# Cached attention, one core: the output projection cut at 24 rows instead of 28, with two transposed tail blocks

## The chip, the cores and the metric

The kernel runs on one core of a Trainium2 chip. The metric is device time in microseconds (us), lower is better: the median of several executions. A profile is one execution recorded instruction by instruction. Engines are named as the profile names them: PE (TensorE, matrix products), PEld (its loads of the stationary operand), DVE (VectorE), ACT (ScalarE), POOL (GpSimd), SP (SyncE, which here issues nearly all DMA transfers). All inputs and the output are bf16; sums are kept in fp32.

## The reference

One new token for each of 32 sequences attends over the last 512 positions of a cache of 2048. There are 32 query heads and 8 key/value heads, so four query heads share one key head.

```python
B, Sq, D = x.shape                 # 32, 1, 512
Hq, Dh = 32, 128
W = min(4096, max(256, Sk // 4))   # 512
q = (x @ wq).reshape(B, Sq, Hq, Dh).transpose(0, 2, 1, 3)
k = jnp.repeat(k_cache[:, :, Sk - W:, :], rep, axis=1)
v = jnp.repeat(v_cache[:, :, Sk - W:, :], rep, axis=1)
p = softmax(einsum("bhqd,bhkd->bhqk", q, k) * Dh ** -0.5)
o = einsum("bhqk,bhkd->bhqd", p, v)
return o.transpose(0, 2, 1, 3).reshape(B, Sq, Hq * Dh) @ wo     # [32, 4096] @ [4096, 512]
```

The last line is the output projection, the part that the change cuts differently. Its contraction is over 4096 = 32 heads of 128, so each row of the output sums 32 products.

## The kernel before, in words

**Data.** One batch's window of keys is 8 heads x 512 positions x 128 numbers, 1 MB; so is its window of values. With 32 batches and two weights of 4 MB the core reads 75.5 MB. SP issues the loads in one written-out order: `k(b)` and `v(b-3)` in turn up to b = 28, with `wo` after b = 10, then `k` of 29 to 31, then `v` of 26 to 31. A key load waits until PE has transposed the keys four batches earlier (four buffers); a value load waits until PE has used the values ten batches earlier (ten buffers). The two output transfers stand behind all of these on SP.

**One batch on PE.** `transposes(b)` turns a batch's keys in 32 products of 128x128 (line 218) into four PSUM banks of `kT_ps`; DVE copies three of the four banks to SBUF and ACT the fourth (lines 416 and 353). `scores(b)` is 8 products of 128x512 (line 234).

**One block is four batches.** The scores of four batches (4 x 32 rows) accumulate in one half of `sc_ps`, the halves taken in turn: even blocks use columns 0 to 511, odd blocks 512 to 1023. When block `kb` is complete, DVE takes its row maximum (`max_block`, lines 438 and 440), ACT the exponential with the row sum (`exp_block`, 365), DVE the reciprocal and the scaling (`norm_block`, 445 and 449), PE transposes the probabilities (`ptrans`, 248), ACT copies them (`pt_evac`, 379), PE multiplies by the values (`pv`, 32 narrow products of 128x4 for each batch, line 263), and DVE copies the block's result to `oT_sb` (`ot_evac`, 456). `oT_sb` holds the attention output transposed: a head's 128 numbers on the partitions, a column for each batch and head.

**The output projection.** Two forms are used. In `oproj_main` (line 279) the attention output is the stationary operand and a head's 128x512 slice of `wo` streams past: 32 products give the first 28 rows of the output directly, in `sc_ps[0:28, 0:512]`. In `oproj_last` (line 292) a 128x128 piece of `wo` is stationary and the last block's 4 columns stream past: 4 x 32 = 128 narrow products give the last 4 rows transposed, in 16 columns of `m_ps`; DVE copies them (466), PE turns them in 4 transposes (302), DVE copies them again (468), and SP writes them out (166).

**Order.** Every engine has its own program, written out by hand; semaphores join them, and an engine stands at a wait until it is met. In PE's loop, step s does `transposes(s+2)`, `scores(s)`, and, where a block is due, `ptrans` and `pv`. The loop runs to s = 27, and the end before the change is lines 317 to 332. Written with T for transposes and S for scores: T30, S28, ptrans(6), S29, pv(6) of batches 0 and 1, T31, S30, pv(6) of batches 2 and 3, S31, `oproj_main`, ptrans(7), pv(7), `oproj_last`. `oproj_main` waits for `ot_evac(6)`, which DVE's program puts behind `max_block(7)` (lines 497 and 498).

Of the kernel before, what the change touches and what calls it, by code (L numbers as in the profile page):

```python
# [5 lines left out]
B = 32  # L6
D = 512
H = 32
G = 8
REP = H // G  # L10
DH = 128
SK = 2048
W = 512
# [9 lines left out]
WO_AFTER = 10  # L23
LAG1 = 1
LAG2 = 2

BF16 = mybir.dt.bfloat16
FP32 = mybir.dt.float32
# [5 lines left out]
def bass_standalone__sliding_block_cached__sampling_kernel(  # L34
# [5 lines left out]
    wo: bass.AP,  # L40
    out: bass.AP,
):
    scale = float(DH) ** -0.5
    with ExitStack() as ctx:
        sb = lambda name, shape, dt: ctx.enter_context(nc.sbuf_tensor(name, shape, dt))
# [14 lines left out]
        oT_sb = sb("oT_sb", [128, B * H], BF16)  # L60
        out_sb = sb("out_sb", [128, D], BF16)
        out_sb2 = sb("out_sb2", [128, D], BF16)
        oT2_sb = sb("oT2_sb", [128, 16], BF16)
        mx = [sb(f"mx{i}", [128, 8], FP32) for i in range(2)]
        nmx = [sb(f"nmx{i}", [128, 8], FP32) for i in range(2)]
        ssum = [sb(f"ssum{i}", [128, 8], FP32) for i in range(2)]
# [44 lines left out]
        @block.sync  # L111
        def _(sp):
            def load_k(b):
                slot = b % NK
                if b >= NK:
                    sp.wait_ge(sem_pe_kT, 4 * (b - NK) + 4)
                src = k_cache[b, :, SK - W:, :].rearrange("g (p r) d -> p g (r d)", p=128)
                dst = kbuf[slot][:, :].rearrange("p (g x) -> p g x", g=G)
                sp.dma_start(dst, src).then_inc(sem_k[slot], 16)  # L119

            def load_v(b):
                slot = b % NV
                if b >= NV:
                    sp.wait_ge(sem_pe_pv, b - NV + 1)
                src = v_cache[b, :, SK - W:, :].rearrange("g (p r) d -> p g (r d)", p=128)
                dst = vbuf[slot][:, :].rearrange("p (g x) -> p g x", g=G)
                sp.dma_start(dst, src).then_inc(sem_v[slot], 16)

            def load_wo():
                sp.wait_ge(sem_pe_misc, 2)  # L130
                sp.wait_ge(sem_act_misc, 2)
                sp.dma_start(
                    wbuf[:, :].rearrange("p (h n) -> p h n", h=H),
                    wo.rearrange("(h p) n -> p h n", p=128),
                ).then_inc(sem_wo, 16)

            NB_LAST = B - 4
            load_k(0)
            sp.dma_start(  # L139
                wbuf[:, :].rearrange("p (t n) -> p t n", t=DT),  # L140
                wq.rearrange("(t p) n -> p t n", p=128),
            ).then_inc(sem_wq, 16)
            order = []
            for b in range(1, NB_LAST + 1):
                order.append(("k", b))
                if b >= VLAG:
                    order.append(("v", b - VLAG))
                if b == WO_AFTER:
                    order.append(("wo", 0))
            for b in range(NB_LAST + 1, B):  # L150
                order.append(("k", b))
            for b in range(NB_LAST + 1 - VLAG, B):
                order.append(("v", b))
            assert len(order) == len(set(order)) == 2 * B
            for kind, b in order:
                if kind == "k":
                    load_k(b)
                elif kind == "v":
                    load_v(b)
                else:  # L160
                    load_wo()
            outv = out.rearrange("b o d -> (b o) d")
            sp.wait_ge(sem_dve_out, 1)
            sp.dma_start(outv[0:NB_LAST, :], out_sb[0:NB_LAST, :]).then_inc(sem_out, 16)
            sp.wait_ge(sem_dve_out, 3)
            sp.dma_start(outv[NB_LAST:B, :], out_sb2[0:B - NB_LAST, :]).then_inc(sem_out, 16)
            sp.wait_ge(sem_out, 32)

        @block.gpsimd
# [12 lines left out]
        def _(pe):  # L182
# [38 lines left out]
            def scores(b):  # L221
                blk, bl = divmod(b, 4)
                half = blk % 2
                if bl == 0:
                    pe.wait_ge(sem_dve_L, blk + 1)
                    if blk == 0:
                        pe.wait_ge(sem_act_misc, 2)
                    if blk >= 2:
                        pe.wait_ge(sem_act_exp, blk - 1)
                for g in range(G):  # L230
                    n = 4 * b + g // 2
                    if g % 2 == 0:
# [36 lines left out]
                            )  # L269
                    ins.then_inc(sem_pe_pv, 1)  # L270

            NB_LAST = B - 4

            def oproj_main():
                pe.wait_ge(sem_dve_oT, NBLK - 1)
                pe.wait_ge(sem_wo, 16)
                pe.wait_ge(sem_act_exp, NBLK - 1)
                for h in range(H):
                    ins = pe.matmul(  # L279
                        sc_ps[0:NB_LAST, 0:512],  # L280
                        bass.AP(oT_sb, h, [[B * H, 128], [H, NB_LAST]]),
                        wbuf[:, h * D:(h + 1) * D],
                        start=(h == 0),
                        stop=(h == H - 1),
                    )
                ins.then_inc(sem_pe_misc, 1)

            def oproj_last():
                pe.wait_ge(sem_dve_oT, NBLK)
                for c in range(4):  # L290
                    for h in range(H):
                        ins = pe.matmul(  # L292
                            m_ps[:, c * 4:(c + 1) * 4],
                            wbuf[:, h * D + c * 128: h * D + (c + 1) * 128],
                            bass.AP(oT_sb, NB_LAST * H + h, [[B * H, 128], [H, B - NB_LAST]]),
                            start=(h == 0),
                            stop=(h == H - 1),
                        )
                ins.then_inc(sem_pe_misc, 1)
                pe.wait_ge(sem_dve_out, 2)  # L300
                for c in range(4):
                    ins = pe.transpose(pT_ps[0:B - NB_LAST, c * 128:(c + 1) * 128], oT2_sb[:, c * 4:(c + 1) * 4], ident[:, :])  # L302
                ins.then_inc(sem_pe_misc, 1)

            xT()
            transposes(0)
            transposes(1)
            qproj()
            for s in range(0, NB_LAST):
                transposes(s + 2)  # L310
                scores(s)
                for kb in range(NBLK - 2):
                    if s == 4 * kb + 3 + LAG1:
                        ptrans(kb)
                    if s == 4 * kb + 3 + LAG2:
                        pv(kb)
            transposes(NB_LAST + 2)
            scores(NB_LAST)
            ptrans(NBLK - 2)
            scores(NB_LAST + 1)  # L320
            pv(NBLK - 2, (0, 1))
            transposes(NB_LAST + 3)
            scores(NB_LAST + 2)
            pv(NBLK - 2, (2, 3))
            scores(NB_LAST + 3)
            oproj_main()
            ptrans(NBLK - 1)
            pv(NBLK - 1, (0,))
            pv(NBLK - 1, (1,))
            pv(NBLK - 1, (2,))  # L330
            pv(NBLK - 1, (3,))
            oproj_last()

        @block.scalar
        def _(act):
# [42 lines left out]
                    act.wait_ge(sem_act_pT, kb - 1)  # L378
                act.activation(pT_sb[kb % 2][:, :], pT_ps[:, 0:W], ACTF.Copy).then_inc(sem_act_pT, 1)  # L379

            def block_tasks_pre(b):
                pass

            def block_tasks_post(b):
                for kb in range(NBLK):
                    if b == 4 * kb + 5:
                        exp_block(kb)
                    if b == 4 * kb + 5 + LAG1:
                        pt_evac(kb)

            xt_evac()
            evac(0, 3)
            evac(1, 3)
            qt_evac()
            for b in range(2, B):
                block_tasks_pre(b)
                evac(b, 3)
                block_tasks_post(b)
            for b in range(B, B + 12):
                block_tasks_pre(b)  # L400
                block_tasks_post(b)

        @block.vector
        def _(dve):
# [50 lines left out]
                reg = kb % 4  # L455
                dve.tensor_copy(oT_sb[:, kb * 128:(kb + 1) * 128], m_ps[:, reg * 128:(reg + 1) * 128]).then_inc(sem_dve_oT, 1)  # L456

            NB_LAST = B - 4

            def out_evac():  # L460
                dve.wait_ge(sem_pe_misc, 3)
                dve.tensor_copy(out_sb[0:NB_LAST, :], sc_ps[0:NB_LAST, 0:512]).then_inc(sem_dve_out, 1)

            def out_last():
                dve.wait_ge(sem_pe_misc, 4)
                dve.tensor_copy(oT2_sb[:, :], m_ps[:, 0:16]).then_inc(sem_dve_out, 1)
                dve.wait_ge(sem_pe_misc, 5)
                dve.tensor_copy(out_sb2[0:B - NB_LAST, :], pT_ps[0:B - NB_LAST, 0:512]).then_inc(sem_dve_out, 1)

            def E(b):  # L470
                for c in range(3):
                    evac(b, c)

            def block_tasks_pre(b):
                for kb in range(NBLK):
                    if b == 4 * kb + 6 and kb <= NBLK - 2:
                        norm_block(kb)
                    if b == 4 * kb + 5 + LAG2 + 1 and kb <= NBLK - 3:
                        ot_evac(kb)

            def block_tasks_post(b):
                for kb in range(NBLK - 1):
                    if b == 4 * kb + 5:
                        max_block(kb)
                for blk in range(1, NBLK):
                    if b == max(2, 4 * blk - 2):
                        lcopy(blk)

            E(0)
            E(1)  # L490
            lcopy(0)
            for b in range(2, B):
                block_tasks_pre(b)
                E(b)
                block_tasks_post(b)
            kb6, kb7 = NBLK - 2, NBLK - 1
            max_block(kb7)
            ot_evac(kb6)
            norm_block(kb7)
            out_evac()  # L500
            ot_evac(kb7)
            out_last()


# [26 lines left out]
```

## Time and profile before

| | |
|---|---|
| median of 6 runs | 235.33 us (234.91 to 237.51) |
| the profiled execution's own time | 236.34 us |
| its span, first to last instruction | 234.2 us |
| mean granted PE clock | 0.85 |
| busy: PE / PEld / DVE / ACT | 176.4 / 137.8 / 78.9 / 46.3 us |
| read from HBM | 75.53 MB, 323 GB/s over the span |
| `oproj_main`: 32 products, start to start of the next work | 215.67 to 222.78 us |
| `oproj_last`: 128 narrow products | 227.65 to 231.24 us |

How to read it: times inside the trace are us from the first instruction. A busy share is an average over the span; the end of this kernel has a limit of its own, so a stage is read by itself. The chain of work that ended last is followed back from the last instruction, at each step to whatever released it. The start and end of PE's instructions overlap, since products are pipelined; the pace of a group is the distance between starts. The granted clock is the share of full speed that PE was given.

### The profile page before, as it was taken

What the parts mean: (1) busy time and instruction counts of PE and PEld (TensorE: products, weight loads), DVE (VectorE), ACT (ScalarE), POOL (GpSimd) and SP (SyncE); (2) the same over time, 40 slices, a digit from 0 to 9 for tenths busy, and PEclk for the clock granted to TensorE, in tenths of its full rate; (3) what the DMA queues carried; (4) which work ended last, traced back from release to release, by engine and by line L of the source; (5) the groups of instructions that cost most, each with busy time, mean ns of one, the idle gap of its engine ahead of it and who ended that gap; (6) DMA issues with size and microseconds to landing.
All of it is one profiled execution on the core that took longest, in us unless ns stands there. A gap on an engine that the chain in (4) does not pass through costs nothing.

```text
span 234.2 us, 5764 instructions
## 1 busy us (share of the span) xinstructions
PE 176.4 (75%) x2609; PEld 137.8 (59%) x2632; DVE 78.9 (34%) x147; ACT 46.3 (20%) x59; POOL 8.2 (4%) x9
## 2 busy tenths in 40 slices
PE   0606799699863029996968679977998699997985
PEld 0506767468641026964846459745875588675575
DVE  0303335442361003444333531553165306632011
ACT  2100232221132001034111410332023101511010
POOL 7600000000000000000000000000000000000000
PEclk9965999899799556799997977997799778999975
DMA  6999999999999999999999999999999999999200
GB/s 230 413 391 348 350 349 349 350 348 350 348 351 348 348 348 350 348 350 348 349 350 348 349 348 349 348 349 348 350 348 348 348 348 347 350 335 345 82 8 4
DMA packets 71306, 75.94 MB, mean 324 GB/s; under 512 B 1090, under 2 KB 70754, under 8 KB 70770
## 3 DMA queue, kind: packets, MB, share of 16 engines
q1 hardware_dynamic: 71250, 75.53, 100.0%
q8 instruction: 21, 0.34, 0.6%
q0 software_dynamic: 32, 0.03, 0.0%
q14 instruction: 3, 0.02, 0.0%
HBM read 75.53 MB, written 0.03 MB: 323 GB/s over the span
## 4 chain that ended last, share of the span: by engine, by line
DMA 51%; PE 42%; issue 3%; DVE 1%; SPq 0%; ACT 0%; DVEq 0%
DMA kbuf<-in_k_cache_dram 51%; PE kT_ps L218 16%; PE sc_ps L234 12%; PE m_ps L263 9%; PE sc_ps L279 3%; PE m_ps L292 2%; PE sc_ps L195 1%; DVE kT L416 1%; DVE mx L438 0%; ACT pT L379 0%; DVE oT_sb L456 0%; PE pT_ps L302 0%; PE pT_ps L248 0%; SPq L139 0%; SPq L119 0%
## 5 line engine op out<-in xcount | busy, mean ns | idle before, releaser
L218 PE MATMUL kT_ps<-ident,kbuf 128*128 128x128 bf16 x1024 | 79.1, 249 | 43.8 <-DMA kbuf<-in_k_cache_dram 42.0
L218 PEld LDWEIGHTS kT_ps<-ident,kbuf 128*128 128x128 bf16 x1024 | 74.0, 114 | 50.5 <-DMA kbuf<-in_k_cache_dram 46.6
L416 DVE COPY kT<-kT_ps 128x1024 bf16<-128x1024 bf16 x96 | 62.4, 686 | 83.0 <-issue 40.2
L234 PE MATMUL sc_ps<-kT,L 128*128 128x512 bf16 x233 | 60.2, 398 | 2.0 <-issue 0.9
L353 ACT ACTIVATE kT<-kT_ps 128x1024 bf16<-128x1024 bf16 x32 | 32.7, 1023 | 140.0 <-PE kT_ps L218 129.1
L234 PEld LDWEIGHTS sc_ps<-kT,L 128*128 128x128 bf16 x256 | 24.9, 103 | 26.2 <-issue 5.5
L263 PEld LDWEIGHTS m_ps<-pT,vbuf 128*128 128x128 bf16 x1024 | 27.2, 97 | 2.7 <-ACT pT L379 0.9
L263 PE MATMUL m_ps<-pT,vbuf 128*128 128x4 bf16 x1024 | 27.2, 165 | 0.7 <-ACT pT L379 0.7
L456 DVE CAST oT_sb<-m_ps 128x128 bf16<-128x128 f32 x8 | 2.3, 292 | 36.1 <-PE m_ps L263 36.1
L438 DVE TENSOR_REDUCE mx<-sc_ps 128x1 f32<-128x512 f32 x8 | 5.5, 692 | 12.8 <-PE sc_ps L234 12.8
L365 ACT ACTIVATE E_sb<-sc_ps,nmx 128x512 f32<-128x512 f32 x8 | 5.5, 687 | 15.9 <-DVE nmx L440 15.9
L279 PE MATMUL sc_ps<-wbuf,oT_sb 128*28 128x512 bf16 x32 | 7.1, 380 | 1.2 <-DVE oT_sb L456 1.2
L379 ACT ACTIVATE pT<-pT_ps 128x512 bf16<-128x512 bf16 x8 | 4.8, 597 | 13.1 <-PE pT_ps L248 13.1
L279 PEld LDWEIGHTS sc_ps<-wbuf,oT_sb 128*28 128x28 bf16 x32 | 3.9, 126 | 4.4 <-DVE oT_sb L456 1.7
L187 PE MATMUL pT_ps<-ident,x_sb 32*128 32x32 bf16 x4 | 0.3, 183 | 7.2 <-DMA x_sb<-in_x_dram 7.2
L187 PEld LDWEIGHTS pT_ps<-ident,x_sb 32*128 32x128 bf16 x4 | 0.2, 101 | 7.2 <-issue 7.2
L449 DVE TENSOR_SCALAR P<-E_sb,rs 128x512 bf16<-128x512 f32 x8 | 3.9, 487 | 0.3
L292 PE MATMUL m_ps<-oT_sb,wbuf 128*128 128x4 bf16 x128 | 3.6, 168 | 0.4 <-DVE oT_sb L456 0.4
L292 PEld LDWEIGHTS m_ps<-oT_sb,wbuf 128*128 128x128 bf16 x128 | 3.5, 103 | 0.5 <-DVE oT_sb L456 0.5
L430 DVE COPY L<-qT_sb 128x128 bf16<-128x128 bf16 x8 | 2.1, 259 | 4.5 <-ACT qT_sb L342 4.5
L248 PEld LDWEIGHTS pT_ps<-ident,P 128*128 128x128 bf16 x32 | 2.4, 98 | 2.1 <-issue 0.4
L445 DVE RECIPROCAL rs<-ssum 128x1 f32<-128x1 f32 x8 | 1.3, 164 | 6.5 <-ACT E_sb L365 6.5
(22 smaller groups left out, 26.1 us busy)
## 6 DMA issues: line engine op xcount, KB each, us to landing
kbuf<-in_k_cache_dram SPq DMA_DIRECT2D x32, 1024.0 KB, 12.0
vbuf<-in_v_cache_dram SPq DMA_DIRECT2D x32, 1024.0 KB, 12.1
wbuf<-in_wq_dram SPq DMA_DIRECT2D x1, 4096.0 KB, 15.2
wbuf<-in_wo_dram SPq DMA_DIRECT2D x1, 4096.0 KB, 20.8
x_sb<-in_x_dram POOLq DMA_DIRECT2D x1, 32.0 KB, 5.9
out_dram<-out_sb SPq DMA_DIRECT2D x1, 28.0 KB
out_dram<-out_sb SPq DMA_DIRECT2D x1, 4.0 KB
```

Of the source, the lines that this page charges most:

```text
L218: ins = pe.transpose(dst, src, ident[:, :])
L234: ins = pe.matmul(sc_ps[:, half * 512:(half + 1) * 512], L[blk % 2][:, (bl * 8 + g) * 128:(bl * 8 + g + 1) * 128], kT_sb[b % NKT][:, g * W ...
L248: ins = pe.transpose(pT_ps[:, j * 128:(j + 1) * 128], P_sb[kb % 2][:, j * 128:(j + 1) * 128], ident[:, :])
L263: ins = pe.matmul(m_ps[:, reg * 128 + bl * 32 + 4 * g: reg * 128 + bl * 32 + 4 * g + 4], vbuf[vslot][:, g * W + j * 128: g * W + (j + 1) * ...
L279: ins = pe.matmul(sc_ps[0:NB_LAST, 0:512], bass.AP(oT_sb, h, [[B * H, 128], [H, NB_LAST]]), wbuf[:, h * D:(h + 1) * D], start=(h == 0), st ...
L292: ins = pe.matmul(m_ps[:, c * 4:(c + 1) * 4], wbuf[:, h * D + c * 128: h * D + (c + 1) * 128], bass.AP(oT_sb, NB_LAST * H + h, [[B * H, 12 ...
L353: act.activation(kT_sb[b % NKT][:, c * 1024:(c + 1) * 1024], kT_ps[:, bank * 1024:(bank + 1) * 1024], ACTF.Copy,).then_inc(sem_act_kT, 1)
L365: act.activation(E_sb[:, :], sc_ps[:, half * 512:(half + 1) * 512], ACTF.Exp, bias=nmx[kb % 2][:, 0:1], scale=1.0, accum_out=ssum[kb % 2][ ...
L379: act.activation(pT_sb[kb % 2][:, :], pT_ps[:, 0:W], ACTF.Copy).then_inc(sem_act_pT, 1)
L416: dve.tensor_copy(kT_sb[b % NKT][:, c * 1024:(c + 1) * 1024], kT_ps[:, bank * 1024:(bank + 1) * 1024],).then_inc(sem_dve_kT, 1)
L438: dve.tensor_reduce(mx[kb % 2][:, 0:1], sc_ps[:, half * 512:(half + 1) * 512], AXX, ALU.max).then_inc(sem_dve_loc, 1)
L449: dve.tensor_scalar(P_sb[kb % 2][:, :], E_sb[:, :], rs[kb % 2][:, 0:1], None, ALU.mult).then_inc(sem_dve_P, 1)
```

## The change

The direct form now makes 24 rows (blocks 0 to 5) and is called `oproj_A`; it writes the other half of `sc_ps` (columns 512 to 1023) and stands on PE right after S27. Blocks 6 and 7 each get the transposed form, `oprojT(6)` and `oprojT(7)`, 128 narrow products each, into 32 columns of `m_ps`; one `out_transposes` turns both together, and the second output transfer carries 8 rows. PE's end becomes T28, S26, S27, `oproj_A`, ptrans(6), pv(6) of batches 0 and 1, T29, S28, T30, T31, S29, S30, S31, pv(6) of batches 2 and 3, `oprojT(6)`, ptrans(7), pv(7), `oprojT(7)`, `out_transposes`. S28 gets one more wait, for DVE's copy of `oproj_A`'s result, since block 7 uses that half of `sc_ps`. On DVE the end is written out: E28 (three bank copies), max and norm of block 6, the copy of `oproj_A`'s result, E29 to E31, `ot_evac(6)`, max and norm of block 7, `ot_evac(7)`. ACT keeps the same operations: E28, exp and probabilities of block 6, E29 to E31, the same for block 7. The order of the loads on SP is the same list as before.

```diff
-        oT2_sb = sb("oT2_sb", [128, 16], BF16)
+        oT2_sb = sb("oT2_sb", [128, 32], BF16)
...
-            sp.dma_start(outv[0:NB_LAST, :], out_sb[0:NB_LAST, :]).then_inc(sem_out, 16)
+            sp.dma_start(outv[0:NB_A, :], out_sb[0:NB_A, :]).then_inc(sem_out, 16)
             sp.wait_ge(sem_dve_out, 3)
-            sp.dma_start(outv[NB_LAST:B, :], out_sb2[0:B - NB_LAST, :]).then_inc(sem_out, 16)
+            sp.dma_start(outv[NB_A:B, :], out_sb2[0:B - NB_A, :]).then_inc(sem_out, 16)
...
+                    if b == NB_A + 4:
+                        pe.wait_ge(sem_dve_out, 1)
...
+            def oproj_A():
+                pe.wait_ge(sem_dve_oT, NB_A // 4)
                 pe.wait_ge(sem_wo, 16)
+                pe.wait_ge(sem_act_exp, NB_A // 4)
                 for h in range(H):
                     ins = pe.matmul(
+                        sc_ps[0:NB_A, 512:1024],
+                        bass.AP(oT_sb, h, [[B * H, 128], [H, NB_A]]),
                         wbuf[:, h * D:(h + 1) * D],
...
+            def oprojT(kb):
+                pe.wait_ge(sem_dve_oT, kb + 1)
+                q = kb - (NBLK - 2)
                 for c in range(4):
                     for h in range(H):
                         ins = pe.matmul(
+                            m_ps[:, c * 8 + 4 * q: c * 8 + 4 * q + 4],
                             wbuf[:, h * D + c * 128: h * D + (c + 1) * 128],
+                            bass.AP(oT_sb, 4 * kb * H + h, [[B * H, 128], [H, 4]]),
...
+            transposes(28)
+            scores(26)
+            scores(27)
+            oproj_A()
+            ptrans(6)
+            pv(6, (0, 1))
+            transposes(29)
+            scores(28)
+            transposes(30)
+            transposes(31)
+            scores(29)
+            scores(30)
+            scores(31)
+            pv(6, (2, 3))
+            oprojT(6)
+            ptrans(7)
+            pv(7, (0,))
...
+            oprojT(7)
+            out_transposes()
...
+            ot_evac(5)
+            E(28)
+            max_block(6)
+            norm_block(6)
+            out_evac_A()
+            E(29)
+            E(30)
+            E(31)
+            ot_evac(6)
+            max_block(7)
+            norm_block(7)
+            ot_evac(7)
             out_last()
```

## The prediction

> **What bounds the kernel now.** I read the page's 40 slices first, because a busy share over the whole span cannot say what bounds the end.
>
> ```profile
> PE   0606799699863029996968679977998699997985
> ...
> PEclk9965999899799556799997977997799778999975
> DMA  6999999999999999999999999999999999999200
> ```
>
> One slice is 5.9 us. The transfers are saturated from slice 1 to slice 36, that is to about 217 us, and PE has holes among them. In slices 32 to 39, about 188 us on, PE shows no low digit. So there may be a handover: transfers set the pace for most of the span, and PE sets it before the transfers have ended. The chain of work that ended last says where. Its last piece of transfer is the key load that releases T27 at 183.76 us; from there to the end every piece is compute (columns: start us, length us, what).
>
> ```profile
> 195.38 1.67 PE sc_ps L234 x7
> 197.06 1.79 PE kT_ps L218 x32
> 198.84 1.73 PE sc_ps L234 x8
> ...
> 214.52 0.70 DVE mx L438
> ...
> 215.67 7.11 PE sc_ps L279 x32
> ...
> 223.80 3.48 PE m_ps L263 x128
> 227.30 0.30 DVE oT_sb L456
> ...
> 227.65 3.59 PE m_ps L292 x128
> ```
>
> The reader is to see that S26, T29 and S27 follow each other without a hole, and that nothing between 195 and 214 us waits for a load: PE is full there, at granted clock 1.00. Idle time of PE begins only after S31, and it is small: 214.49 to 215.67 (DVE's maximum, its negation and ot_evac(6)), then 223.12 to 223.80 (ACT's copy of the probabilities), then 227.28 to 227.65 (ot_evac(7)). The chain also has a piece of 2.13 us called "issue" at 206.05, which would be a hole if it were empty. The timeline (start, length, engine, line, operation) shows PE at work in it:
>
> ```profile
> 205.87 1.75 PE L263 MATMUL m_ps<-pT,vbuf 128*128 128x4 bf16 x64
> ```
>
> and the 32 products of T31 start at 207.48. It is not idle time.
>
> **The move of the large block.** oproj_main costs 7.11 us for 32 products of 512 columns, 222 ns each. oproj_A has the same 32 products with 24 instead of 28 stationary columns. Their loads take 125 ns (line 279's weight loads, median) and lie under the 222 ns, so I give the smaller block no gain: 7.11 us leaves the tail and 7.11 us enters between S27 and ptrans(6). Its waits are met there: block 5's exp and ot_evac (192.38 to 192.67 us) are long done at 198.8 us. PE has no hole to put it in, so all that follows, T29 to S31 and pv(6), starts 7.11 us later than its own work would allow. **Cost 0.** The cover that could make it a gain would be PE waiting for keys 29 to 31 in that stretch; no such wait is recorded before T29, T30 or T31.
>
> **The second tail block.** oprojT(6) is new work on PE: 128 products like line 292's, while row count in the direct form fell without making it shorter. Line 292 took 3.59 us for 128, at clock 0.50. The same shape in pv(6) at clock 1.00 took 1.58 us for 64, that is 3.16 us for 128. Ends 3.16 and 3.59; it starts around 223 us, and in the run of before the clock fell at 225.4, so I take **+3.5**.
>
> **The wait after ptrans(6).** Before, ACT's copy of block 6's probabilities lay beside S29 (1.74 us) and PE did not stand. Now pv(6) follows ptrans(6) at once. The row for it is the same step of block 7: 223.12 to 223.80, 0.02 + 0.60 + 0.05. Queued behind pv(6) on PE are T29 and everything to the end. **+0.67.** With something put between, it would be 0.
>
> **The wait before oprojT(6).** It needs ot_evac(6), which needs the end of pv(6). The row is ot_evac(7), 227.28 to 227.65: **+0.39** (its idle time on PE in the timeline; 0.37 by the chain).
>
> **The wait that goes.** After S31 PE stood 214.49 to 215.67, **-1.18**. Late next is block 7's softmax, which DVE now starts only after ot_evac(6). From the start of the maximum (214.52) to the end of the scaling (216.44 + 0.49 = 216.93) it takes 2.41 us. Counted from the end of pv(6): 0.35 + 2.41 = 2.8 us, against 0.39 + 3.5 = 3.9 us until oprojT(6) ends. So it is hidden by oprojT(6) with 1.1 us to spare; without that cover ptrans(7) would stand for up to 2.8 us.
>
> **DVE and ACT around the moved block.** DVE's copy of oproj_A's result (0.68 us, line 462's row) now stands ahead of E29 to E31, and DVE waits at it for oproj_A. Behind it wait T30 and S29 at most; it ends about 206.6 us by my schedule, and T29's first bank is complete only after 208.9. S28's new wait is for the same copy and is met 3 us earlier. T30 and T31 now come back to back: six DVE copies of 0.63 us (1.89 for three), 3.8 us, against 3.6 to 3.9 us of transposes, with S29 needing E29 only. **0**, between 0 and 0.4. The first output transfer moves to about 207 us, but on SP it still stands behind the last value load; 24 KB at the 349 GB/s of those slices is 0.07 us, and pv(7) starts some 6 us after the transfers have faded (slices of 0.5 us: 0.22 at 218.5, then almost nothing). **0**; if a load had to wait for it, 0.07.
>
> **The end.** oT2 is 32 columns instead of 16: line 456 takes 292 ns for 128 columns and line 466 about 177 for 16, a slope of 1 ns, so +0.02. The 4 KB transfer becomes 8 KB; the tail from its issue to the end is 234.2 - 232.56 = 1.6 us for 4 KB and I give the other 4 KB nothing (a gain is excluded, the amount is twice; a loss is at most 0.02 at 349 GB/s). ptrans(7) follows some 6 us of narrow products instead of the wide oproj_main, so it may find the clock at 0.50, as the last four transposes did (0.60 us against 0.35): **+0.2**, with pv(7)'s first half, between 0 and 0.4.
>
> **Code.** PE gets 256 more instructions. The trace has one stall inside a group of transposes without a releaser, 1.82 us at 27.74 us, right after the 128 products of the query projection. The nearest rows, pv(7) and oproj_last with 128 products each, have none. I take 0, between 0 and 1.82.
>
> **Sum:** 3.5 + 0.67 + 0.39 - 1.18 + 0.02 + 0.2 = **+3.6 us**. On the profiled execution's own time, 236.34, this gives 239.9; that execution stands 1.0 above the median of the runs, so on 235.33 it gives **238.9**.
>
> **The clock.** The granted clock moves in steps of 3.41 us. The rows are windows cut on those steps (PE busy, PEld, DVE, ACT, POOL, then granted clock, DMA share, GB/s):
>
> ```profile
> 112.80:116.21 3.41, 3.36 (x97) 2.76 (x96) 0.22 (x1) 0.69 (x1) 0.00 (x0) 1.00 1.09 349
> 116.21:119.62 3.41, 3.36 (x79) 3.06 (x77) 2.06 (x4) 0.44 (x1) 0.00 (x0) 1.00 1.12 353
> ...
> 187.89:191.30 3.41, 3.36 (x100) 2.82 (x100) 0.00 (x0) 0.00 (x0) 0.00 (x0) 1.00 1.10 348
> 191.30:194.72 3.42, 3.42 (x65) 3.42 (x62) 1.60 (x3) 0.00 (x0) 0.00 (x0) 0.50 1.10 348
> ...
> 222.02:225.43 3.41, 2.72 (x73) 2.06 (x72) 0.68 (x1) 0.60 (x1) 0.00 (x0) 1.00 0.03 8
> 225.43:228.85 3.42, 3.03 (x114) 2.95 (x112) 0.29 (x1) 0.00 (x0) 0.00 (x0) 0.50 0.02 5
> ```
>
> Narrow products and idle time together fill 2.27 us of the window at 112.80 (pv starts at 113.94) and the clock stays. They fill 2.36 us at 187.89 (pv from 188.94) and 2.3 us at 222.02 (0.68 idle, pv from 223.80), and it falls to 0.50 for the next step. In the new order ptrans(6)'s wait and pv(6) of two batches make 0.67 + 1.6 to 1.75, about 2.3 to 2.4 us, between oproj_A and T29. That is at the boundary, and only if one window holds all of it. By the phase of this run a step would end at 208.37 and hold about 2.1 of it. If the clock falls, T29 and S28 run at half speed for one step, at most 3.41 / 2 = 1.7 us. I take 0, with 1.7 as the far end.
>
> [...]
>
> **The rivals.** (a) As summed, 238.9 us: chance 0.66. (b) The clock falls after pv(6), 238.9 + 1.5 = 240.4 us (T29 at up to 3.60 us, as the transposes at 86.48 in the chain, instead of 1.79; the cap of 1.7 for one step, less a little for a step that ends or begins in other work): for it the 2.3 against 2.27 us; against it that the phase must fit, (3.41 - 2.35) / 3.41 = 0.3. Chance 0.22. (c) Part of the chain's "issue" piece is real idle time that the new order fills: 238.9 - 2.1 = 236.8 us; against it the 64 products recorded there. Chance 0.05. (d) Faster, by one mechanism: in 195 to 214 us PE in truth stands for keys 29 to 31, and oproj_A lies beside that wait. If all 7.11 us are hidden, 238.9 - 7.1 = 231.8 us; it decides the sign as soon as 3.6 us are hidden. For it: transfers run at 348 GB/s to 216 us. Against it: clock 1.00 with PE busy 4.95 of 5 us at 195 to 200 and 200 to 205. Chance 0.04. (e) The change does nothing that can be measured, its added work eaten by the 1.18 us and a shorter oproj_A: it would need 24 stationary columns to cost 3.6 us less than 28. Chance 0.03.
>
> **How the numbers follow.** About 0.5% (1.2 us) is what a measurement of this kernel can tell from no change. Slower: (a) + (b) + (c) = 0.93 ((c) lies 0.6% above). Faster: (d) 0.04. Same: (e) 0.03. The low end of (a) has oprojT(6) at 3.16 and the clock effect of the end at 0: 3.16 + 0.67 + 0.39 - 1.18 = 3.0, and from it the spread of the runs below their median (0.42) is taken: 237.9. The high end takes in (b) with its far end 1.7: 235.33 + 5.3 = 240.6, and 0.1 for the stalls bounded above. The range 237.9 to 240.7 leaves out (c), (d) and (e), 0.12.
>
> **What the next profile would show.** Right: in the chain, line of oproj_A directly after S27 at about 199 us with no hole before it; PE idle about 0.67 us before pv(6) and 0.4 before oprojT(6); oprojT twice, 256 products; S31 ending about 6.2 us later than 214.49 (7.11 + 0.67, less the 1.6 of pv(6) that now follows it); the last DVE copy about 3.6 us later. Wrong: holes of PE before T29 to T31 that end on a load (then (d)); T29 at 3 us or more (then (b)); ptrans(7) waiting for DVE's scaling (then the cover of block 7's softmax is gone, up to 2.8 us more).

## The result and the profile after

The changed kernel is slower: 240.65 us median (239.55 to 242.17) against 235.36 us, a ratio of 1.022 (95% interval 1.018 to 1.026). A second comparison gave 239.96 against 235.45 us, 1.0186 (1.0136 to 1.0236). So the change costs 4.5 to 5.3 us. The forecast was 238.9 us with a range of 237.9 to 240.7.

The profiled execution took 240.36 us, with a span of 237.3 us. Its slices (5.9 us each) that answer to those shown of before:

```profile
PE   0606699669952049966976699669886999899985
...
PEclk9999999997999558998899997999599999979855
DMA  7999999999999999999999999999999999998000
```

The transfers end in the same place, at about 218 us. In the stretch where PE is full, from about 190 us on, one slice of the clock stands out: a 7 in slice 35 (207.7 to 213.6 us), which the windows below resolve. (The 5 in slice 28, from 166 us, lies ahead of T27.) The chain of waits of the changed kernel from the large block on (start us, length us, what):

```profile
196.33 7.04 PE sc_ps L280 x32
203.36 0.34 PE pT_ps L251 x4
203.71 0.02 issue
203.73 0.61 ACT pT L390
204.34 0.05 issue
204.38 1.76 PE m_ps L266 x64
206.14 2.55 PE kT_ps L219 x32
208.68 0.22 issue
208.91 2.42 PE sc_ps L237 x7
...
220.08 1.60 PE m_ps L266 x64
221.68 0.02 issue
221.70 0.30 DVE oT_sb L464
222.01 0.05 issue
222.05 3.55 PE m_ps L294 x128
```

The reader is to see five things. The large block now stands at 196 us and is as long as before (7.04 against 7.11 us). After ptrans(6) PE waits 0.67 us for ACT's copy. Before the new 128 products it waits 0.37 us for DVE's copy. The new products take 3.55 us. And T29 and S28 take 2.55 and 2.42 us, where the kernel before had 1.79 and 1.68 us for the same work. The windows of the changed kernel, cut at the steps of the clock (PE busy, PEld, DVE, ACT, POOL, granted clock, DMA share, GB/s), show why:

```profile
203.59:207.00 3.41, 2.72 (x84) 2.62 (x83) 0.79 (x2) 0.60 (x1) 0.00 (x0) 1.00 1.09 348
207.00:210.42 3.42, 3.20 (x21) 2.22 (x20) 1.58 (x3) 1.02 (x1) 0.00 (x0) 0.50 1.06 344
210.42:213.83 3.41, 3.41 (x52) 2.95 (x51) 1.96 (x4) 0.62 (x1) 0.00 (x0) 1.00 1.05 344
```

The first window holds the 0.69 us of idle time and the narrow products of pv(6) whole, and the clock is 0.50 for the step that follows.

### The profile page after: what moved, and what is told of

The parts are those of the page before. It is cut to its first block, busy times and chain, and to the rows that moved or that the text cites. A ratio compares the mean times of both kernels' runs of the same rounds, so it can differ in the third digit from the quotient of the medians.

```text
span 237.3 us, 6022 instructions
## 1 busy us (share of the span) xinstructions
PE 174.2 (73%) x2738; PEld 135.1 (57%) x2760; DVE 78.4 (33%) x147; ACT 46.4 (20%) x59; POOL 8.2 (3%) x9
## 4 chain that ended last, share of the span: by engine, by line
DMA 56%; PE 37%; issue 3%; DVE 2%; ACT 1%; SPq 0%; DVEq 0%
DMA kbuf<-in_k_cache_dram 56%; PE kT_ps L219 11%; PE sc_ps L237 11%; PE m_ps L266 8%; PE m_ps L294 3%; PE sc_ps L280 3%; PE sc_ps L196 1%; DVE kT L424 1%; ACT pT L390 1%; PE pT_ps L251 0%; DVE oT_sb L464 0%; PE pT_ps L306 0%; SPq L140 0%; SPq L121 0%; DVE out_sb L474 0%
## 5 line engine op out<-in xcount | busy, mean ns | idle before, releaser
L219 PE MATMUL kT_ps<-ident,kbuf 128*128 128x128 bf16 x1024 | 73.6, 239 | 49.2 <-DMA kbuf<-in_k_cache_dram 46.7
L219 PEld LDWEIGHTS kT_ps<-ident,kbuf 128*128 128x128 bf16 x1024 | 68.2, 108 | 56.6 <-DMA kbuf<-in_k_cache_dram 52.4
L424 DVE COPY kT<-kT_ps 128x1024 bf16<-128x1024 bf16 x96 | 61.6, 686 | 86.5 <-issue 38.1
L237 PE MATMUL sc_ps<-kT,L 128*128 128x512 bf16 x234 | 58.6, 391 | 1.9 <-issue 0.4
L294 PE MATMUL m_ps<-oT_sb,wbuf 128*128 128x4 bf16 x256 | 7.1, 168 | 0.8 <-DVE oT_sb L464 0.8
L294 PEld LDWEIGHTS m_ps<-oT_sb,wbuf 128*128 128x128 bf16 x256 | 7.0, 101 | 0.9 <-DVE oT_sb L464 0.9
L280 PE MATMUL sc_ps<-wbuf,oT_sb 128*24 128x512 bf16 x32 | 7.1, 380 | 0.0
L280 PEld LDWEIGHTS sc_ps<-wbuf,oT_sb 128*24 128x24 bf16 x32 | 3.7, 119 | 3.3 <-issue 0.4
L179 POOL MEMSET L<- 128x4096 bf16 x1 | 3.5, 3507 | 0.0
L180 POOL MEMSET L<- 128x4096 bf16 x1 | 3.5, 3507 | 0.0
```

What stands on the lines that cost most here:

```text
L179: pool.memset(L[0][:, :], 0.0).then_inc(sem_pool, 1)
L219: ins = pe.transpose(dst, src, ident[:, :])
L237: ins = pe.matmul(sc_ps[:, half * 512:(half + 1) * 512], L[blk % 2][:, (bl * 8 + g) * 128:(bl * 8 + g + 1) * 128], kT_sb[b % NKT][:, g * W ...
L280: ins = pe.matmul(sc_ps[0:NB_A, 512:1024], bass.AP(oT_sb, h, [[B * H, 128], [H, NB_A]]), wbuf[:, h * D:(h + 1) * D], start=(h == 0), stop= ...
L294: ins = pe.matmul(m_ps[:, c * 8 + 4 * q: c * 8 + 4 * q + 4], wbuf[:, h * D + c * 128: h * D + (c + 1) * 128], bass.AP(oT_sb, 4 * kb * H + ...
L424: dve.tensor_copy(kT_sb[b % NKT][:, c * 1024:(c + 1) * 1024], kT_ps[:, bank * 1024:(bank + 1) * 1024],).then_inc(sem_dve_kT, 1)
```

## The experiments

All times below are medians, with the ratio to the kernel before, measured beside it, and its 95% interval.

| kernel | us | ratio | interval |
|---|---|---|---|
| changed, again | 239.96 | 1.0186 | 1.0136 to 1.0236 |
| wait after ptrans(6) filled | 238.97 | 1.0131 | 1.0077 to 1.0186 |
| T29 into that wait | 238.37 | 1.0098 | 1.0063 to 1.0133 |
| T29 into that wait, and pv(5) cut in two | 238.23 | 1.0088 | 1.0053 to 1.0123 |
| T29 ahead of S27, T30 into that wait | 239.24 | 1.0159 | 1.0138 to 1.0181 |
| one tail block | 240.51 | 1.0173 | 1.0115 to 1.0230 |
| one tail block, maximum first | 237.12 | 1.0079 | 1.0050 to 1.0109 |
| before, again | 235.57 | 1.0004 | 0.9987 to 1.0021 |
| before, waits filled | 233.93 | 0.9933 | 0.9907 to 0.9959 |
| all rows transposed | 235.02 | 0.9974 | 0.9957 to 0.9991 |
| all rows transposed, columns side by side | 231.43 | 0.9811 | 0.9778 to 0.9844 |

**Both kernels once more.** No edit.

> The changed kernel once more, beside the three variants of it. Theory A (PE is full from T27 on; +3.5 for the second tail block, +0.67 and +0.39 for two new waits, -1.18 for the one that goes; the rest is the PE clock, which falls in some executions after pv(6)): about 240.6 us, and in its trace T29 and S28 take 3.5 us in an execution where the clock stays and up to 5.2 where it falls. Rival R (the whole difference of 5.3 us is work and waits, the clock has no part): 240.6 us, and the trace shows a further wait of 1 us or more that the sum did not have.

> The kernel before once more, for a second trace and its clocks. Theory A: 235.4 us; the steps of 3.41 us at which the clock changes lie elsewhere against the kernel's start than in the first trace, and the number of steps at 0.50 between T27 and S31 (two in the first trace) differs. Rival: the steps lie where they lay.

The second trace of the changed kernel again has a step at half clock from about 206.7 us, with T29 and S28 at 2.56 and 2.64 us, 5.20 together as theory A had it, and no further wait of 1 us, which rival R asked for. The second trace of the kernel before has the clock at 1.00 from T27 to 227 us, and there it shows what the first trace had hidden. PE's timeline in it (idle time and its releaser in brackets):

```profile
191.17 1.95 PE L218 MATMUL kT_ps<-ident,kbuf 128*128 128x128 bf16 x32
193.16 1.67 PE L234 MATMUL sc_ps<-kT,L 128*128 128x512 bf16 x7
196.37 1.96 PE L218 MATMUL kT_ps<-ident,kbuf 128*128 128x128 bf16 x32 [1.53 <-DMA kbuf<-in_k_cache_dram]
```

T29 waits 1.53 us for its keys. In the first trace two steps at half clock (184.47 to 187.89 and 191.30 to 194.72 us) had slowed T27, S25 and T28 so far that T29 came after its keys, so that execution showed no wait. Two variants below that keep the order of this stretch, "all rows transposed" in both layouts, show the same wait for key load 29 in their traces, 1.52 and 1.56 us. With the two second traces the account can be closed, both counted from the start of T27 (184.43 and 183.88 us) to the end of the span: 49.15 us before and 53.14 us after, 3.99 us more.

| term | before, again | changed, again | us |
|---|---|---|---|
| oprojT(6) | none | 221.75 to 225.29 | +3.55 |
| wait after ptrans(6) | beside S29 | 203.40 to 204.07 | +0.67 |
| wait for ot_evac(6) ahead of oprojT(6) | none | 221.37 to 221.75 | +0.38 |
| wait after S31 | 213.98 to 215.15 | none | -1.17 |
| T29 and S28 | 1.79 + 1.72 | 2.56 + 2.64 | +1.69 |
| ptrans(7), pv(7), last copy | 0.34 + 3.37 + 0.18 | 0.46 + 3.59 + 0.20 | +0.36 |
| wait of T29 for key load 29 | 1.53 | none | -1.53 |
| sum | | | +3.95 |

**The clock after pv(6).**

```diff
             ptrans(6)
+            for _ in range(12):
+                pe.matmul(
+                    m_ps[:, 0:128], kT_sb[0][:, 0:128], kT_sb[0][:, 128:256],
+                    start=True, stop=True,
+                )
             pv(6, (0, 1))
```

> The changed kernel with 12 products of 128x128 (56 ns each, 0.67 us) put into the wait between ptrans(6) and pv(6); their result is used by nobody. Idle time and narrow products ahead of T29 shrink from 2.35 to about 1.7 us in one stretch. Theory A: no work is taken away and the wait is only filled, but the clock no longer falls for T29: 0 to 1.7 us less than the changed kernel, by how often it fell, about 1 us in the median, 239.6 us. Rival R: the same time as the changed kernel within 0.3 us, or a little more.

238.97 us, 1.0 less than the changed kernel measured beside it; no work was taken away. The intervals of the two ratios overlap, so the trace has to carry it. The chain of this variant:

```profile
204.74 0.67 PE m_ps L328 x12
205.41 0.02 issue
205.43 1.76 PE m_ps L266 x64
207.18 1.81 PE kT_ps L219 x32
208.99 1.73 PE sc_ps L237 x8
```

The 12 products take the place of the wait, 0.67 us for 0.67 us, and T29 and S28 are back at 1.81 and 1.73 us. In this execution T28 met a slow step instead (3.06 us), so one trace could owe its fast T29 to where the steps happened to lie. All traces together leave little room for that: in the four in which pv(6) of two batches follows the wait (two of the changed kernel, and the two one-tail variants below) the step after it is slow every time, and in the four in which the wait is filled (this one and the three variants with T29 or T30 in it) never. So the clock falls after ptrans(6) and pv(6) because of the stretch with little wide work, and the price of one step in T29 and S28 is 1.7 us (5.20 us for the two against 1.79 + 1.72).

**The wait itself.**

```diff
             ptrans(6)
+            transposes(29)
             pv(6, (0, 1))
-            transposes(29)
             scores(28)
```

> The changed kernel with T29 moved between ptrans(6) and pv(6) of batches 0 and 1. Theory A: ACT's copy (0.67 us) lies beside T29, and the stretch without wide products shrinks to 1.6 us, so the clock stays: 0.67 + about 1 = 1.7 us less than the changed kernel, 239.0 us. Rival R: 0.67 less, 240.0 us. If the wait had cost nothing: 240.6 us.

238.37 us, 1.6 less than the changed kernel, where theory A had 1.7 and the rival 0.67. In the chain pv(6) follows T29 without a piece of ACT between them:

```profile
204.51 0.33 PE pT_ps L251 x4
204.84 1.79 PE kT_ps L219 x32
206.62 1.58 PE m_ps L266 x64
```

**Where the other slow steps come from.** The executions of the changed kernel fall into groups by span: 236.8 to 237.3 us (5 of 12), 238.4 to 238.6 (5) and 239.9 to 240.0 (2). The distance is about 1.4 us, near one slow step. None lies near 235.4 us, the shortest of the variant with the wait filled, so each of the 12 seems to carry at least one slow step. Of the kernel before, the great majority lie between 232.8 and 233.8 us. The last variant had one execution at 234.5 and six at 236.0 to 236.4 us. I took the remaining slow step for an effect of pv(5), and cut that in two, on top of the last variant:

```diff
+            pv(5, (0, 1))
+            scores(26)
+            pv(5, (2, 3))
             transposes(28)
-            scores(26)
             scores(27)
```

> The variant with T29 between ptrans(6) and pv(6), and in addition pv(5) cut in two with S26 between its halves, so that no 128 narrow products follow one another between T27 and S31; the work is the same. Theory A (what is over the sum is the clock: steps of 3.41 us at 0.50 between T27 and S31, each paid in full because PE meets no load there): the variant without this cut has one such step in most executions (spans 236.0 to 236.4) and none in one (span 234.5); now nearly all lie at the latter, 236.7 us, 1.7 us below that variant's 238.4, with little spread. Rival R (the spread is something else): 238.4 us, as the variant without the cut.

This failed: 238.23 us, six executions at 236.0 to 236.4 and two at 234.7 us. In its trace T28 is fast, but the slow step has moved to T27, whose line in the chain reads

```profile
183.83 3.56 PE kT_ps L219 x32
```

against 1.96 us in the second trace of either kernel. Ahead of T27 PE waits 2.12 us for key load 27, and that wait may have lowered the clock here, as a stretch with pv(5) in it may have in the first trace of before (2.36 us of pv(5) in the window from 187.89 us, then a step at 0.50); the second traces of both kernels have the same wait, 2.12 and 2.11 us, and no slow T27. The step costs 3.56 - 1.96 = 1.6 us here, near the distance between the groups, but pv(5) was not its only source; no execution of the group at 234.7 was traced.

**Whether a load behind it absorbs a slow step.** From the second pair of traces I formed a new theory: the kernel before can take a slow step at T27 or T28 for nothing, since PE has to wait for key load 29 anyway; the changed kernel has no such wait left and pays in full.

```diff
             scores(26)
+            transposes(29)
             scores(27)
             oproj_A()
             ptrans(6)
-            transposes(29)
+            transposes(30)
             pv(6, (0, 1))
             scores(28)
-            transposes(30)
             transposes(31)
...
             E(28)
+            E(29)
             max_block(6)
             norm_block(6)
             out_evac_A()
-            E(29)
             E(30)
```

> The variant with T29 between ptrans(6) and pv(6) is changed once more: T29 goes to its old place between S26 and S27, ahead of the large block, and T30 takes its place between ptrans(6) and pv(6). The work is the same, but PE now meets key load 29 (landed about 196.3 us) after T27, as it does in the kernel before. Theory A2 (formed after the runs so far: in most executions of the kernel before PE waits about 1.5 us for key load 29, which the changed kernel fills with the large block, and a step at half clock between T27 and T29 is absorbed by that wait in the kernel before but paid in full in the changed one): spans of 236.0 to 236.4 in nearly all executions, whether a step falls there or not, 238.2 us, and no execution at 234.5. Rival (the steps cost the same with or without that load wait): two groups as in the variant without it, 236.2 and 234.5, or all of them 1.5 us higher.

239.24 us: four executions at 236.5 to 236.7 us and two at 237.8 to 238.0, none at 234.5. The group at 234.5 is gone and the spread has shrunk at its fast side, as the theory says, but the spans of the lower group are 0.4 us over what I expected, the median is 1.0 us over it, and two executions lie higher. The profiled one is of those two: it has two slow steps (about 185.3 to 188.7 and 192.1 to 195.5 us), and T29 started at 197.72, after its keys. The runs agree with the theory, but two groups 1.5 us higher (236.0 and 237.7), a form of the rival, lie as near; since no trace of the lower group was taken, these runs do not settle it. The two traces of the kernel before say more. Counted from the start of T27, the two slow steps of the first put the end of S26 2.9 us later than in the second (13.3 against 10.4 us), but the start of T29 only 1.4 us later (13.3 against 11.9) and the end of the kernel 1.3 us later (50.45 against 49.15). The wait for key load 29 took up the other 1.5 us.

**The second tail block.** Both tails in one, 8 columns, after pv(7); 128 products in place of 256:

```diff
             pv(6, (2, 3))
-            oprojT(6)
             ptrans(7)
...
             pv(7, (3,))
-            oprojT(7)
+            oprojT(6)
...
-                            m_ps[:, c * 8 + 4 * q: c * 8 + 4 * q + 4],
+                            m_ps[:, c * 8: c * 8 + 8],
-                            bass.AP(oT_sb, 4 * kb * H + h, [[B * H, 128], [H, 4]]),
+                            bass.AP(oT_sb, 4 * kb * H + h, [[B * H, 128], [H, 8]]),
```

> The changed kernel with one transposed tail block of 8 columns for blocks 6 and 7 after pv(7), 128 narrow products in place of 256; DVE's order is left, so block 7's maximum still stands behind ot_evac(6). Theory A: 3.55 + 0.39 us of PE go, but oprojT(6) was what hid block 7's softmax, and ptrans(7) now stands until 2.8 us after pv(6): net -1.1 us, 239.5 us. Rival (the softmax is not what is late next): -3.9 us, 236.7 us.

The median is 240.51 us, with executions from 237.93 to 241.3, and does not tell this from the changed kernel. The profiled executions, this one and the second trace of the changed kernel, can be compared, since one slow step met T29 and S28 in both (5.18 and 5.20 us for the two): the spans are 235.8 and 237.0 us, 1.2 less, where 1.1 was expected and the rival had 3.9. Why four of the six executions lie 2 to 3.4 us higher in span was not traced. The timeline shows the wait that took the place of the block:

```profile
223.85 0.61 PE L251 MATMUL pT_ps<-ident,P 128*128 128x128 bf16 x4 [2.70 <-DVE P L455]
```

With DVE's order changed as well:

```diff
+            max_block(7)
             ot_evac(6)
-            max_block(7)
             norm_block(7)
```

> The one-tail variant (128 narrow products for blocks 6 and 7 together) with DVE taking block 7's maximum before ot_evac(6). Theory A: the softmax of block 7 now runs from the end of S31, 2.45 us, of which pv(6) of two batches (1.6 us) covers the most: 3.94 - 0.85 = 3.1 us less than the changed kernel, 237.5 us. So with the second tail block gone, most of the loss is gone. Rival R2 (the loss comes from the early place of the large block and not from the second tail block): no more than 1.1 us less, 239.5 us.

237.12 us; by the ratios to the kernel before (1.0079 against 1.0186) 2.5 us less than the changed kernel, where 3.1 was expected and the rival allowed 1.1. The wait of ptrans(7) is down from 2.70 to 0.98 us:

```profile
222.36 0.40 PE L251 MATMUL pT_ps<-ident,P 128*128 128x128 bf16 x4 [0.98 <-DVE P L455]
```

So 2.5 of the changed kernel's 4.4 us go with the second block, once block 7's softmax no longer waits behind ot_evac(6); the early place of the large block alone does not explain the loss.

**Filling the waits of the kernel before.** Its end, reordered:

```diff
-            scores(NB_LAST + 2)
             pv(NBLK - 2, (2, 3))
+            scores(NB_LAST + 2)
             scores(NB_LAST + 3)
-            oproj_main()
+            oproj_main(0, 12)
             ptrans(NBLK - 1)
+            oproj_main(12, 30)
...
             pv(NBLK - 1, (3,))
+            oproj_main(30, 32)
             oproj_last()
...
+            ot_evac(kb6)
             max_block(kb7)
-            ot_evac(kb6)
             norm_block(kb7)
-            out_evac()
             ot_evac(kb7)
+            out_evac()
```

> The kernel before, with its 28 rows and one tail block; only the order of the end is changed: pv(6) of batches 2 and 3 ahead of S30, ot_evac(6) ahead of block 7's maximum, and the 32 products of the large block laid around ptrans(7) (12 before, 18 after) and behind pv(7) (2). Theory A (PE is full, only its three waits can be won): -1.18 - 0.67 - 0.37 = -2.2 us, 233.1 us. Rival: the waits are replaced by others (a value load, the scaling), 235.4 us.

233.93 us, faster than before by 0.7% (0.4 to 0.9%), 1.4 us of the 2.2 expected. All three waits are gone from the chain:

```profile
214.87 2.73 PE sc_ps L280 x12
217.60 0.33 PE pT_ps L248 x4
217.93 4.02 PE sc_ps L280 x18
221.95 3.29 PE m_ps L263 x128
225.24 0.57 PE sc_ps L280 x2
225.81 3.51 PE m_ps L294 x128
```

The large block in three pieces takes 2.73 + 4.02 + 0.57 = 7.32 us, 0.2 more than in one. In the profiled execution T29 also came at 197.45 us, after two slow steps, 1.1 us later than in the second trace of before. Three of the six executions lie at 231.3 to 231.5 us in span, 1.7 to 1.9 below the usual 233.2 of the kernel before, so the short executions reach most of the 2.2 us. The rest of the shortfall I did not trace.

**One transposed block for all rows.** Since a narrow product seems to cost by its number (28 ns each with 4 and with 8 columns, at clock 0.50), the wide form may not be needed at all:

```diff
-            pv(NBLK - 2, (2, 3))
             scores(NB_LAST + 3)
-            oproj_main()
+            pv(NBLK - 2, (2, 3))
...
-                            m_ps[:, c * 4:(c + 1) * 4],
+                            m_ps[:, c * 32:(c + 1) * 32],
-                            bass.AP(oT_sb, NB_LAST * H + h, [[B * H, 128], [H, B - NB_LAST]]),
+                            bass.AP(oT_sb, h, [[B * H, 128], [H, B]]),
```

> The kernel before with the large block left away: one transposed block of 128 products with 32 columns for all rows after pv(7), then four transposes and one output transfer of 32 rows; pv(6) of batches 2 and 3 behind S31. Theory A (PE is full, and a product of few columns costs by its number, not by its columns; 128 products of 128x32 of the query projection took 3.3 us): -7.1 for the large block, -1.2 for its wait, +0.85 for ptrans(7) waiting for block 7's softmax, +0.3 for wider copies: -7 us, 228.3 us; if pv(7)'s last batch then waits for the last value load (landed about 220 us), -6 us, 229.3 us. Rival (32 columns cost as much as the wide form): no change or slower.

235.02 us: 0.3% faster, not 3%; the time is the rival's. The expectation's wait for the last value load is there, but the block itself is more than twice as long as expected. The timeline:

```profile
220.69 1.01 PE L261 MATMUL m_ps<-pT,vbuf 128*128 128x4 bf16 x32 [1.68 <-DMA vbuf<-in_v_cache_dram]
...
222.09 7.46 PE L277 MATMUL m_ps<-oT_sb,wbuf 128*128 128x32 bf16 x128 [0.38 <-DVE oT_sb L440]
```

58 ns for a product against 28 ns with 4 columns at the same clock. The 32 columns of a head lie 64 bytes apart in this layout. No run so far told whether that distance costs anything with 32 columns, so the next one laid the columns side by side, by a strided write in ot_evac:

```diff
-                dve.tensor_copy(oT_sb[:, kb * 128:(kb + 1) * 128], m_ps[:, reg * 128:(reg + 1) * 128])
+                dve.tensor_copy(
+                    bass.AP(oT_sb, 4 * kb, [[B * H, 128], [1, 4], [B, H]]),
+                    m_ps[:, reg * 128:(reg + 1) * 128].rearrange("p (b h) -> p b h", b=4),
+                )
...
-                            bass.AP(oT_sb, h, [[B * H, 128], [H, B]]),
+                            oT_sb[:, h * B:(h + 1) * B],
```

> The one transposed block for all 32 rows, with the attention output laid out so that the 32 columns of a head lie side by side (before: 64 bytes apart). Theory A (in the variant with columns apart the 128 products took 7.47 us, 58 ns each, because of the distance between columns and the clock at 0.50 together; the query projection's 128 products with 32 columns side by side took 3.3 us): the block takes 3.4 to 3.7 us, 235.0 - 3.8 = 231.2 us. Rival (the clock alone makes it 58 ns): 235.0 us, no change.

231.43 us, 1.9% faster than the kernel before (1.6 to 2.2%), and the best of all. The timeline:

```profile
221.95 0.71 DVE L440 CAST oT_sb<-m_ps 128x128 bf16<-128x128 f32 x1 [7.11 <-PE m_ps L261]
222.72 3.60 PE L277 MATMUL m_ps<-oT_sb,wbuf 128*128 128x32 bf16 x128 [0.81 <-DVE oT_sb L440]
```

The block takes 3.60 us, 28 ns each, the same as with 4 columns; the price is DVE's copy, 0.72 in place of 0.29 us. The rival (the clock alone) has fallen: the clock was 0.50 in both for the whole block. So with 32 columns it was the distance of 64 bytes that cost, 58 against 28 ns; with 4 or 8 columns the same distance shows no cost (28 ns each). In this version PE waits again for the last value load (1.68 us at 220.90), so the end hangs on the transfers, and its executions lie within 0.9 us of each other.

## Why the prediction was right, and where it was not

The direction, the size within the range and the main mechanism held: a second transposed block that nothing covers. That the size fell within the range is in part luck. The median of 240.65 us lies 0.05 below the upper end, which reaches so far only because it takes in the far end of rival (b); the case summed as (a), 238.9 us with a chance of 0.66, is not what the traces show, since the clock did fall after pv(6). Term by term:

- **The second tail block**, forecast +3.5: 3.55 us. Right.
- **The wait after ptrans(6)**, +0.67: 0.67 us. **The wait before oprojT(6)**, +0.39: 0.38 us. **The wait that goes**, -1.18: -1.17 us. All right, each read off the same step of another block.
- **The cover of block 7's softmax**, "up to 2.8 us" if oprojT(6) were not there: with that block away, ptrans(7) stood 2.70 us. Right.
- **The end**, +0.2: +0.36 us. ptrans(7) and pv(7) met the lower clock as foreseen; pv(7) lost 0.22 us of it.
- **DVE, ACT, the output transfer, the code**, 0: T30 and T31 back to back took 3.57 us, which is two times 1.79; no stall without a releaser of the length bounded there is in the chain. Right.
- **The move of the large block at cost 0**: wrong, and so was the statement under it that PE has no hole to put it in. In the traces without slow steps ahead of it, PE stands 1.52 to 1.56 us before T29 for key load 29, and the large block fills that. It is the mechanism of rival (d), at 1.53 of the 7.11 us, where 3.6 were needed to turn the sign. The trace that I had could not show it, because two slow steps ahead of T29 had used that wait up. The same two steps were in the windows that I quoted; I read them for a threshold and not for what they did to T29.
- **The clock, taken at 0 with 1.7 as the far end**: wrong as a value. The drop after pv(6), rival (b), is in both traces of the changed kernel and costs 1.69 us there. I gave it 0.22 because the 3.41 us window would have to fit the stretch. The sign that I named for it, T29 at 3 us or more, did not show, because T29 (2.55 us) and S28 (2.42 us) shared the step. The threshold read from the windows (2.3 us without wide products) held where the window has narrow products: in the first trace of the changed kernel 2.26 us from 186.52 us on did not bring the clock down, and 2.31 us from 203.59 us on did. It does not hold for idle time alone: in the kernel before, the window from 181.06 to 184.47 us, with 2.12 us of idle time and no narrow products, was followed by a step at 0.50.

The two errors have opposite signs and nearly cancel in the traced pair (-1.53 and +1.69). What is over in the medians, 4.5 to 5.3 us against the 3.95 of the pair, goes with the executions that lie one or two groups higher. That these have a slow step at T27 or T28 as well, which the kernel before loses in its wait for key load 29, fits the spans and the trial with T29 first; it was not shown in a trace of such an execution. Without any slow step the change would cost about 3.6 - 1.5 = 2.1 us: the two shortest executions of the variant with the wait filled, 235.4 and 235.6 us in span, stand 2.2 to 2.4 over the usual 233.2 of the kernel before.

## What to carry to other kernels

Cut an output projection by the number of products and not by the number of rows: here 128 products with 4, 8 or 32 columns took 3.6 us alike at half clock, the 32 only when they lay side by side, so every further block of that form was a full price, and one block for all rows was the fastest of the variants. Read whether an engine is full from more than one execution: slow steps of the clock can use up a wait (here the 1.53 us ahead of T29), and then the trace shows an engine without room where there is some. Where a chain has a load to wait for behind it, slow steps can vanish in that wait (1.5 of 2.9 us in the kernel before); a reordering that removes the wait can make them count.

## What the runs showed of the hardware that I had not expected

- The clock fell after a window in which PE issued without long gaps. The longest idle time in the window from 203.59 us was 0.69 us, beside narrow products of 128x4, and the next 3.41 us were at 0.50. In the first trace of before, 2.12 us of idle time without narrow products (window from 181.06 us) were followed by a step at 0.50 as well; in the second, the same 2.12 us ahead of T27 were not.
- The steps of the clock do not lie on one grid from kernel start to kernel start: it fell at 225.43 us in the first trace of before and at about 227.25 us in the second, 1.8 us apart, where whole steps are 3.41 us.
- A streamed operand with 32 columns 64 bytes apart made a 128x32 product take 58 ns in place of 28 ns at the same clock (0.50); with 4 or 8 columns the same distance cost nothing that shows (28 ns each).
- DVE's copy of 128x128 from PSUM with a write of 64 bytes' step took 0.72 us in place of 0.29 us.
